# A new order of the opening in a fused linear-attention and feed-forward kernel: two row blocks of w_in ahead of the last pair's loads, and the first q on another queue

## The chip, the cores and the metric

The kernel runs on one NeuronCore of a Trainium2 chip. The metric is the device time of one launch in microseconds (us); lower is better. The kernel before takes 258.86 us, the median of three runs (258.49 to 258.88). Engines are named as the profile names them: PE is TensorE (PEld its weight loads), DVE is VectorE, ACT is ScalarE, POOL is GpSimd, and SP is the engine that does nothing here but issue DMAs.

## The reference, and what is computed

Eight batches of eight heads, 576 rows of 64 elements each, go through a linear attention without softmax; its output is normalised per row and head, and the 4608 rows of 512 go through a two-layer feed-forward net with a gate:

```
kv  = einsum('bhsd,bhse->bhde', k, v)            # 64 x 64 for each head
out = einsum('bhsd,bhde->bhse', q, kv)
x   = out / sqrt(mean(out * out, -1) + 1e-6) * g_norm
h   = x @ w_in                                   # 512 -> 2048
g   = h * sigmoid(1.702 * h)
y   = g @ w_out                                  # 2048 -> 512
```

Inputs and output are f32. The kernel computes in f16 with f32 accumulation in PSUM.

## The kernel before, in words

**Tiles and layers.** The order of all instructions is written out by hand: each engine runs its instructions in program order, and the framework adds the semaphore waits that the data and the buffers need. A batch's 512 features are four *pairs* of heads (128 rows of x each, `NPAIR` = `KO` = 4). The hidden layer of one batch is 16 column blocks of 128 (`FO`), and each is a sum of four matmuls, one for each row block of w_in, that is, one for each pair: `d0.mm(ko, fo)` multiplies row block `ko` of column block `fo` with `x` of pair `ko`, 512 tokens wide (L478). `gate(fo)` then applies the gated activation on ScalarE (L487). The first batch's sixteen columns run in the order `COLS` = 0-3, 8-11, 4, 5, 6, 12, 13, 7, 14, 15. After them `project_all` multiplies with w_out (L822). The later batches (from 46 us on) use a scheme of seven products in place of eight for both layers (L589, L709); the change doesn't touch them.

**The opening.** Batch 0 is not turned by DMA as later ones are, but worked pair by pair. For pair `c`: `q(c)` transposes q on TensorE (twelve small matmuls, L439) and VectorE copies the result out (L445); `kv(c)` forms K transposed times V (twelve matmuls, L261) and VectorE masks it into `kvb` (L429); `out(c)` multiplies both (L307) and ScalarE squares the result (L325, the tile `sq`); `ss(c)` sums the squares over each head with a matmul by ones (L384) and ScalarE takes the reciprocal root (L386, the tile `rs`); `apply(c)` multiplies out, rs and g_norm on VectorE into x (L394). Then the hidden matmuls of row block `c` can run. `busy(n)` issues n matmuls whose result nobody reads (L869). The list of calls from `a0 = First(0)` on (L858 to L923) sets the order on all engines.

**The group.** Hidden matmuls can't be finished before the last pair's x is there. So `GROUP` = 6 columns are begun early, each in a PSUM bank of its own (three of the pool `ps_h`, one of `ps_a`, two of `ps_o`): their row blocks 0 to 2 run while pair 3 is still on its way, then row block 3 and the gate follow for all six. The other ten columns run one after another in banks of `ps_h` (`first_columns`, L804), with other work hung on the positions 6, 7, 8, 12 and 13 of the column order.

**Queues.** Pair 0's k, q and v are loaded as f32 by three DMAs on SP's queue (L161) and cast by DVE, ACT and DVE; the small g_norm comes by ScalarE's queue. All else is loaded by POOL's queue, which casts to f16 on the way: q, k, v of pairs 1, 2, 3 (`early_load`, L91), then w_in in eight DMAs (`load_w_in(f0, f1, k0, k1)`: column blocks f0 to f1 of row blocks k0 to k1, L180), then w_out (L206) and batch 1. The order on this queue is the order of the calls.

Of the kernel before, what the change touches and what calls it, by code (L numbers as in the profile page):

```python
# [7 lines left out]
F16 = mybir.dt.float16  # L8
# [4 lines left out]
P = 128  # L13
# [3 lines left out]
def kernel(  # L17
# [10 lines left out]
    nc = tc.nc  # L28

    B, H, S, D = q.shape  # L30
    DM = H * D
    DFF = moe_w_in.shape[1]
    NPAIR = H // 2
    FO = DFF // P
    KO = DM // P
# [6 lines left out]
    EARLY = 2  # L42
    PE_ = 96
    NJ = S // PE_
    GROUP = 6
    COLS = (0, 1, 2, 3, 8, 9, 10, 11, 4, 5, 6, 12, 13, 7, 14, 15)
    assert PE_ * NJ == S and PE_ % 32 == 0

# [7 lines left out]
    ps_a = ctx.enter_context(tc.tile_pool(name="ps_a", bufs=3, space=bass.MemoryType.PSUM))  # L56
    ps_h = ctx.enter_context(tc.tile_pool(name="ps_h", bufs=3, space=bass.MemoryType.PSUM))
    ps_o = ctx.enter_context(tc.tile_pool(name="ps_o", bufs=2, space=bass.MemoryType.PSUM))
# [28 lines left out]
    def early_src(n, b, c0, c1):  # L87
        return srcs[n][b, 2 * c0 : 2 * c1].rearrange("h (p j) d -> p h (j d)", j=NJ)

    def early_load(n, b, c0, c1):  # L90
        nc.gpsimd.dma_start(  # L91
            out=raw[n][0:PE_, c0:c1, :].rearrange("p c (l x) -> p (c l) x", l=2),
            in_=early_src(n, b, c0, c1),
        )
# [60 lines left out]
    for n in "kqv":  # L155
        if n != "q":
            rows = stage.tile([P, 6, 2 * P], F32, name="qf", tag="qf", bufs=2)
            rows = rows.rearrange("p h x -> p (h x)")[0:PE_]
        first[n] = rows[:, (n == "q") * 2 * NJ * D :][:, 0 : 2 * NJ * D]
        dst, src = first[n].rearrange("p (h x) -> p h x", h=2), early_src(n, 0, 0, 1)  # L160
        nc.sync.dma_start(out=dst, in_=src)  # L161
    g_row = const.tile([1, D], F32)
    nc.scalar.dma_start(out=g_row, in_=g_norm.unsqueeze(0))
    nc.vector.memset(ident, 0.0)
# [2 lines left out]
        out=ident,  # L167
        in_=ident,
# [10 lines left out]
    def load_w_in(f0, f1, k0=0, k1=KO):  # L179
        nc.gpsimd.dma_start(  # L180
            out=w_in_sb[:, k0:k1, f0 * P : f1 * P],
            in_=moe_w_in[k0 * P : k1 * P, f0 * P : f1 * P].rearrange(
                "(ko ki) f -> ki ko f", ki=P
            ),
        )

    for c in range(1, NPAIR):
        for n in "qkv":
            early_load(n, 0, c, c + 1)
    load_w_in(0, 4, 0, 1)  # L190
    load_w_in(0, 4, 1, 2)
    load_w_in(0, 4, 2, 3)
    load_w_in(8, 10)
    load_w_in(0, 4, 3, KO)
    load_w_in(10, 12)
    load_w_in(4, 8)
    load_w_in(12, FO)

    nc.scalar.preload_act_table_set("abs_reciprocal_sqrt_and_small")
    nc.vector.memset(eps_t, EPS)  # L200
# [220 lines left out]
    class First(Early):  # L421
# [10 lines left out]
                ones2.rearrange("p (l d) -> p l d", l=2),  # L432
            )

        def q(self, c):
            t = ps_h.tile([P, S], F16, name="q0", tag="hT")
            for j in range(NJ):
                for hl in range(2):
                    nc.tensor.transpose(  # L439
                        t[hl * D : (hl + 1) * D, j * PE_ : (j + 1) * PE_],  # L440
                        qraw[0:PE_, c, (hl * NJ + j) * D : (hl * NJ + j + 1) * D],
                        ident[0:PE_, 0:PE_],
                    )
            s = attn.tile([P, S], F16, name="qT", tag="qT", bufs=4)
            nc.vector.tensor_copy(s, t)  # L445
            self.qT[c] = s
# [340 lines left out]
    def layers(t, units1, units2):  # L787
        hid = d0 if t == 0 else Hidden(t)
        seven = Seven(t, hid.gT) if t else None
        left = hid_seven(t, hid, seven, units1) if t else first_columns(hid, units1)  # L790
        osbs[t] = opool.tile([P, 4, DM], F32, name="osb", tag="osb")
        if t:
            todo = {n: [lambda x=x: seven.sums(*x) for x in xs] for n, xs in plan(t).later.items()}
            for n, us in units2.items():
                todo.setdefault(n, []).extend(us)
            for n, us in left.items():
                todo[n] = us + todo.get(n, [])
            seven.run(todo)
        else:
            project_all(hid.gT, units2)  # L800
        if EARLY <= t < B and t not in HALVED:
            store(t, 0, J)

    def first_columns(hid, units):  # L804

        for i, fo in enumerate(COLS):
            if i >= GROUP:
                for ko in range(KO):
                    hid.mm(ko, fo)
                hid.gate(fo)  # L810
            for u in units.get(i, ()):
                u()
# [45 lines left out]
    a0 = First(0)  # L858
# [8 lines left out]
    def busy(n):  # L867
        for _ in range(n):
            nc.tensor.matmul(  # L869
                idle_ps,  # L870
                kvb[1][:, 0, :],
                kvb[1].rearrange("p c r -> p (c r)"),
                start=True,
                stop=True,
            )
# [14 lines left out]
    a0.kv(1)  # L890
    a0.ss(0)
    a0.out(1)
    a0.q(2)
    busy(1)
    a0.kv(2)
    a0.ss(1)
    a0.apply(0)
    a0.out(2)
    a0.q(3)
    a0.apply(1)  # L900
    d0 = Hidden(0)
    busy(3)
    a0.kv(3)
    a0.ss(2)
    a0.apply(2)
    d0.mm(0, 0)
    d0.mm(0, 1)
    a0.out(3)
    d0.mm(0, 2)
    d0.mm(0, 3, ps_a, "att")  # L910
    for fo in range(4):
        d0.mm(1, fo)
        if fo == 1:
            a0.ss(3)
            a0.apply(3)
    for fo in range(4):
        d0.mm(2, fo)
    for fo in COLS[4:GROUP]:
        for ko in range(KO - 1):
            d0.mm(ko, fo, ps_o, "o")  # L920
    for fo in COLS[0:GROUP]:
        d0.mm(KO - 1, fo)
        d0.gate(fo)  # L923
# [197 lines left out]
```

## Time and profile before

| | before |
|---|---|
| median of three runs | 258.86 us (258.49 to 258.88) |
| span of the profiled execution, first to last instruction | 256.5 us |
| own time of the profiled execution | not listed beside the three runs; the median is 2.4 us above its span |
| PE busy | 250.5 us (98%) |
| DVE, ACT, POOL busy | 194.4, 177.0, 57.8 us |
| granted TensorE clock over the span | 1.000 |
| moved by DMA | 35.33 MB, 138 GB/s in the mean |

In the profile a row of the timeline gives start and length in us, the engine, the line, the operation, out<-in, the shape, how many instructions were merged, and in brackets the idle time before it with what ended that. A row of DMA issues gives the size of one and the median time from issue to landing; asked for a stretch that holds a single issue, it is that one's time. The length of a matmul includes its pipeline: one of 512 columns shows as 0.38 while the next can start 0.216 us after it. In the chain of work that ended last each piece is what the end had to wait for, and lines of TensorE there mean that TensorE itself was the bound.

### The profile page before, as it was taken

To read this page: it belongs to the slowest core of one execution; us is meant where nothing else is said; L and a number is where in the kernel's file an instruction comes from. 1 tells how busy PE (TensorE), PEld (TensorE's weight loads), DVE (VectorE), ACT (ScalarE), POOL (GpSimd) and SP (SyncE) were. 2 spreads that over 40 slices of the span, in tenths; PEclk is the share of its full clock that TensorE was granted. 3 is DMA by queue.
4 is the path that set the end of the run, shared out by engine and by line. 5 is a ranking of instruction groups with operands and counts; after the bars stand their busy time and mean duration, and the time that the engine had idled before them with its cause. 6 is when DMAs were issued, how large, how long until landed. Compare 5 with 4: busy or idle time off the path is not lost.

```text
span 256.5 us, 6359 instructions
## 1 busy us (share of the span) xinstructions
PE 250.5 (98%) x2600; PEld 203.8 (79%) x2600; DVE 194.4 (76%) x341; ACT 177.0 (69%) x322; POOL 57.8 (23%) x94
## 2 busy tenths in 40 slices
PE   7899999999999999999999999999999999999994
PEld 2444544788888888888888888888888889888883
DVE  1557585999958895989588867986899687857872
ACT  3469725978759885989598958995798569537800
POOL 8882155404080104301340143000000000000013
PEclk9999999999999999999999999999999999999999
DMA  7999999998999989998999699909500730012005
GB/s 180 189 201 205 205 204 196 191 178 128 165 183 214 118 115 172 216 273 109 211 170 137 87 228 128 177 4 156 184 4 0 93 155 3 0 75 91 3 19 146
DMA packets 68703, 35.33 MB, mean 138 GB/s; under 512 B 37986, under 2 KB 66274, under 8 KB 68418
## 3 DMA queue, kind: packets, MB, share of 16 engines
q0 software_dynamic: 37648, 18.31, 55.4%
q1 hardware_dynamic: 30624, 16.29, 28.7%
q8 instruction: 20, 0.33, 0.6%
q10 hardware_dynamic: 402, 0.33, 0.4%
q14 instruction: 9, 0.07, 0.1%
HBM read 36.70 MB, written 9.44 MB: 180 GB/s over the span
## 4 chain that ended last, share of the span: by engine, by line
PE 94%; DMA 2%; POOL 2%; DVE 0%; issue 0%
PE o L709 38%; PE h L589 38%; PE o L822 5%; PE hT L478 5%; DMA vbuf<-in_v_dram 2%; PE kvp L248 2%; PE outR L337 1%; PE ss L384 1%; POOL qraw L91 1%; PE outT L307 1%; POOL kraw L91 0%; PE q L459 0%; PE kvp L261 0%; PE idle L869 0%; PE kv L261 0%; PE outT L311 0%
## 5 line engine op out<-in xcount | busy, mean ns | idle before, releaser
L566 ACT ACTIVATE gT<-h 128x512 f16<-128x512 f32 x96 | 52.4, 602 | 5.7 <-PE h L589 5.7
L589 PEld LDWEIGHTS <-ws 128*128 128x128 f16 x512 | 50.0, 98 | 6.0
L709 PEld LDWEIGHTS <-gS 128*128 128x128 f16 x512 | 49.0, 98 | 6.2 <-DVE gS L641 0.3
L589 PE MATMUL h<-xS,ws 128*128 128x256 f16 x384 | 52.2, 273 | 0.0
L709 PE MATMUL o<-tw,gS 128*128 128x256 f16 x384 | 45.6, 273 | 0.0
L589 PEld LDWEIGHTS <-w_in_sb 128*128 128x128 f16 x384 | 37.5, 98 | 4.7
L709 PEld LDWEIGHTS <-gT 128*128 128x128 f16 x384 | 37.6, 98 | 4.3
L709 PE MATMUL o<-w_out_sb,gT 128*128 128x256 f16 x256 | 31.4, 273 | 0.0
L589 PE MATMUL h<-xT,w_in_sb 128*128 128x256 f16 x224 | 31.1, 272 | 0.0
L603 DVE TENSOR_TENSOR h<-h,s 128x512 f32<-128x512 f32 x32 | 22.3, 698 | 4.4 <-PE h L589 2.8
L605 DVE TENSOR_TENSOR s<-h,s 128x512 f32<-128x512 f32 x32 | 22.1, 691 | 4.3 <-PE h L589 3.5
L686 DVE TENSOR_TENSOR osb<-o,qf 128x512 f32<-128x512 f32 (+1 forms) x25 | 16.7, 668 | 11.2 <-PE o L709 11.1
L743 POOL DMA_DIRECT2D out_dram<-osb x6 | 3.2, 538 | 93.2 <-DVE osb L686 93.2
L641 DVE TENSOR_TENSOR gS<-gT 128x512 f16<-128x512 f16 (+2 forms) x32 | 21.3, 684 | 0.6 <-ACT gT L566 0.6
L566 ACT ACTIVATE gT<-s 128x512 f16<-128x512 f32 x32 | 19.8, 628 | 2.8 <-DVE s L605 2.8
L589 PE MATMUL h<-xS,w_in_sb 128*128 128x256 f16 x128 | 18.9, 273 | 0.0
L353 DVE TENSOR_REDUCE sum<-sq 128x8 f32<-128x512 f16 x24 | 14.9, 679 | 4.7 <-ACT sq L347 4.7
L995 ACT ACT_TABLE_LOAD x14 | 18.0, 1283 | 0.3
L535 DVE COPY s<-h 128x512 f32<-128x512 f32 x19 | 13.0, 685 | 6.5 <-PE h L589 6.4
L325 ACT ACTIVATE sq<-outT 128x512 f16<-128x512 f32 (+1 forms) x16 | 7.8, 493 | 14.3 <-PE outT L307 8.7
L115 POOL DMA_DIRECT2D kraw<-in_k_dram x7 | 6.0, 855 | 49.1 <-PE kvp L248 32.5
L386 ACT ACTIVATE rs<-ss,eps_t 128x512 f32<-128x512 f32 (+1 forms) x16 | 9.2, 581 | 11.2 <-PE ss L384 11.2
(105 smaller groups left out, 372.2 us busy)
## 6 DMA issues: line engine op xcount, KB each, us to landing
out_dram<-osb SPq DMA_DIRECT2D x8, 512.0 KB, 5.4
kraw<-in_k_dram POOLq DMA_DIRECT2D x5, 512.0 KB, 6.0
vbuf<-in_v_dram POOLq DMA_DIRECT2D x5, 512.0 KB, 10.0
out_dram<-osb SPq DMA_DIRECT2D x2, 1024.0 KB, 4.1
qraw<-in_q_dram POOLq DMA_DIRECT2D x3, 512.0 KB, 11.0
qbuf<-in_q_dram POOLq DMA_DIRECT2D x3, 512.0 KB, 12.8
out_dram<-osb SPq DMA_DIRECT2D x6, 192.0 KB, 6.7
w_in_sb<-in_moe_w_in_dram POOLq DMA_DIRECT2D x2, 512.0 KB, 9.6
```

The lines of the kernel that those rows point to most:

```text
L353: nc.vector.tensor_reduce(out=self.sum4[:, j, :], in_=self.o[j][1].rearrange("p (x d) -> p x d", d=D), op=ALU.add, axis=mybir.AxisListType.X,)
L478: nc.tensor.matmul(self.h[fo], w_in_sb[:, ko, fo * P : (fo + 1) * P], self.x[:, ko], start=(ko == 0), stop=(ko == KO - 1),)
L535: (nc.vector.tensor_copy if engine == "D" else nc.scalar.copy)(to, src)
L566: nc.scalar.activation(self.gT[:, to, n * TH : (n + 1) * TH], src, AFT.Gelu_apprx_sigmoid)
L589: nc.tensor.matmul(bank[name][:, a], w, x, start=(p in (1, 5) and a == 0 and k == 0), stop=(k == KH - 1), skip_group_check=True,)
L603: nc.vector.tensor_add(bank["z"], bank["x"], self.s5)
L605: nc.vector.tensor_add(self.s5, bank["x"], self.s5)
L641: op(s[:, n, lo], a, b)
L686: nc.vector.tensor_add(o, ps, self.kept[with_][:, m])
L709: nc.tensor.matmul(o, a, w, start=(p in (1, 2, 5) and i == 0 and (mo == 0 or split)), stop=(i == HF - 1), skip_group_check=True,)
L822: nc.tensor.matmul(os[mo], gT[:, fo, mo * P : (mo + 1) * P], w_out_sb[:, fo, :], start=(fo == 0), stop=(fo == FO - 1),)
L995: u2.setdefault(i, []).append(lambda: f(*args))
```

## The change

Six things change, all in the first batch:

- q of pair 0 is asked for on ScalarE's queue instead of SP's, so that k and v alone are on SP's.
- On POOL's queue, row blocks 0 and 1 of w_in's first four columns go ahead of q, k, v of pair 3 instead of behind them.
- The rest of w_in is cut otherwise: columns 8 to 11 come in four DMAs of one row block (before, two DMAs of all four row blocks for two columns each), with row block 3 of the first four columns between the third and fourth; columns 4 to 7 and 12 to 15 come in two DMAs of two row blocks each (before, one each). w_in takes twelve DMAs instead of eight.
- The calls of the opening stand in another order: `apply(0)` and `apply(1)` one step earlier, `kv(3)` and `out(3)` behind hidden matmuls of row blocks 0, 1 and in part 2, and the four fillers `busy(1)` and `busy(3)` are gone; `q(3)` uses a bank of `ps_o`.
- `GROUP` is 7: seven columns have their row blocks 0 to 2 done before row block 3 of any. The banks are three of `ps_h`, two of `ps_a`, two of `ps_o`.
- Positions 9 and 10 of the column order (`MORE`) use banks of `ps_o`.

What is computed stays the same.

```diff
-    GROUP = 6
+    GROUP, MORE = 7, (9, 10)
...
-        nc.sync.dma_start(out=dst, in_=src)
+        (nc.scalar if n == "q" else nc.sync).dma_start(out=dst, in_=src)
...
     for c in range(1, NPAIR):
+        if c == NPAIR - 1:
+            load_w_in(0, 4, 0, 1)
+            load_w_in(0, 4, 1, 2)
         for n in "qkv":
             early_load(n, 0, c, c + 1)
-    load_w_in(0, 4, 0, 1)
-    load_w_in(0, 4, 1, 2)
     load_w_in(0, 4, 2, 3)
-    load_w_in(8, 10)
+    for k0 in range(KO - 1):
+        load_w_in(8, 12, k0, k0 + 1)
     load_w_in(0, 4, 3, KO)
-    load_w_in(10, 12)
-    load_w_in(4, 8)
-    load_w_in(12, FO)
+    load_w_in(8, 12, 3, KO)
+    for f0 in (4, 12):
+        load_w_in(f0, f0 + 4, 0, 2)
+        load_w_in(f0, f0 + 4, 2, KO)
...
-        def q(self, c):
-            t = ps_h.tile([P, S], F16, name="q0", tag="hT")
+        def q(self, c, pool=ps_h, tag="hT"):
+            t = pool.tile([P, S], F16, name="q0", tag=tag)
...
             if i >= GROUP:
+                pool = (ps_o, "o") if i in MORE else (ps_h, "hT")
                 for ko in range(KO):
-                    hid.mm(ko, fo)
+                    hid.mm(ko, fo, *pool)
                 hid.gate(fo)
...
     a0.out(1)
+    a0.apply(0)
     a0.q(2)
-    busy(1)
+    a0.ss(1)
     a0.kv(2)
-    a0.ss(1)
-    a0.apply(0)
-    a0.out(2)
-    a0.q(3)
-    a0.apply(1)
     d0 = Hidden(0)
-    busy(3)
-    a0.kv(3)
-    a0.ss(2)
-    a0.apply(2)
     d0.mm(0, 0)
     d0.mm(0, 1)
-    a0.out(3)
+    a0.out(2)
+    a0.apply(1)
     d0.mm(0, 2)
     d0.mm(0, 3, ps_a, "att")
-    for fo in range(4):
+    d0.mm(1, 0)
+    a0.ss(2)
+    a0.q(3, ps_o, "o")
+    for fo in range(1, 4):
         d0.mm(1, fo)
-        if fo == 1:
-            a0.ss(3)
-            a0.apply(3)
+    a0.apply(2)
+    a0.kv(3)
     for fo in range(4):
         d0.mm(2, fo)
-    for fo in COLS[4:GROUP]:
-        for ko in range(KO - 1):
-            d0.mm(ko, fo, ps_o, "o")
+        if fo == 1:
+            a0.out(3)
+    d0.mm(0, COLS[4], ps_o, "o")
+    d0.mm(0, COLS[5], ps_a, "att")
+    a0.ss(3)
+    a0.apply(3)
+    for ko in range(1, KO - 1):
+        for fo in COLS[4:6]:
+            d0.mm(ko, fo)
+    for ko in range(KO - 1):
+        d0.mm(ko, COLS[6], ps_o, "o")
     for fo in COLS[0:GROUP]:
         d0.mm(KO - 1, fo)
         d0.gate(fo)
```

## The prediction, made before the changed kernel was run

> **What bounds the kernel now.** I read the page first, then busy time by stretch, then the chain of work that ended last, then the timeline of each engine over the first 30 us. The page and the stretches:
>
> ```profile
> span 256.5 us, 6359 instructions
> PE 250.5 (98%) x2600; PEld 203.8 (79%) x2600; DVE 194.4 (76%) x341; ACT 177.0 (69%) x322; POOL 57.8 (23%) x94
> PEclk9999999999999999999999999999999999999999
> ...
> 9.40:13.80 4.40, 3.87 (x56) 1.88 (x56) 2.68 (x6) 2.35 (x4) 3.80 (x6) 1.00 1.28 199
> 13.80:28.20 14.40, 14.40 (x71) 6.51 (x71) 9.37 (x17) 11.53 (x20) 6.65 (x10) 1.00 1.30 203
> 28.20:46.20 18.00, 18.00 (x146) 8.90 (x145) 11.87 (x27) 10.03 (x16) 8.16 (x12) 1.00 1.34 201
> ```
>
> (In a row by stretch: from:to, its length, then PE, PEld, DVE, ACT, POOL busy us, the granted clock, the DMA share, GB/s.) TensorE is full from 13.8 us on. So the change can only win what the time before 13.8 wastes, and can lose if it opens a hole after it. The chain at the joint:
>
> ```profile
> 5.28 5.54 DMA vbuf<-in_v_dram
> ...
> 15.71 5.62 PE hT L478 x26
> ...
> 21.45 6.95 PE hT L478 x32
> 28.40 1.08 PE o L822 x5
> ```
>
> V of pair 2 lands at 5.28 + 5.54 = 10.82 and starts the full stretch; a hidden-layer matmul costs 5.62 / 26 = 0.216 us. TensorE's timeline:
>
> ```profile
> 9.45 0.39 PE L307 MATMUL outT<-qT,kvb 128*128 128x512 f16 x1
> ...
> 10.15 0.39 PE L869 MATMUL idle<-kvb 128*128 128x512 f16 x1
> 10.95 0.38 PE L261 MATMUL kv<-vbuf,kraw 96*64 96x64 f16 x12 [0.42 <-DMA vbuf<-in_v_dram]
> ...
> 12.41 0.82 PE L869 MATMUL idle<-kvb 128*128 128x512 f16 x3
> ...
> 13.81 0.61 PE L478 MATMUL hT<-xT,w_in_sb 128*128 128x512 f16 x2
> ...
> 15.54 5.79 PE L478 MATMUL hT<-xT,w_in_sb 128*128 128x512 f16 x26
> ```
>
> The first hidden matmul starts at 13.81. Two, then four, then a run of 26 from 15.54: the 22nd is the 16th of that run, at 15.54 + 15 x 0.217 = 18.79. After it 42 more follow without a hole. This 22nd is my yardstick: in the changed order it is the first that needs the last pair's x (21 products of three row blocks with seven column blocks come before it), and 43 remain from it in either kernel.
>
> **The change part by part.** *The DMA order.* Landings, from issue plus time to landing, one answer for each issue:
>
> ```profile
> 7.14 0.64 POOL L91 DMA_DIRECT2D vbuf<-in_v_dram  x1
> 7.76 1.13 POOL L180 DMA_DIRECT2D w_in_sb<-in_moe_w_in_dram  x2
> 9.53 0.53 POOL L180 DMA_DIRECT2D w_in_sb<-in_moe_w_in_dram  x1 [0.64 <-DMA qraw<-in_q_dram]
> ...
> vbuf<-in_v_dram POOLq DMA_DIRECT2D x1, 144.0 KB, 5.9
> ...
> w_in_sb<-in_moe_w_in_dram POOLq DMA_DIRECT2D x1, 128.0 KB, 6.0
> ...
> w_in_sb<-in_moe_w_in_dram POOLq DMA_DIRECT2D x1, 128.0 KB, 5.4
> ```
>
> Pair 3's V lands at 7.14 + 5.9 = 13.04, so its three loads took (13.04 - 10.82) / 3 = 0.74 each. The first w_in block lands at 13.76 (0.72 behind), the third at 14.93, so 0.59 for each of the next two. With two blocks ahead: first block 11.55, second 12.13, pair 3's V 12.13 + 2.22 = 14.35, third block 14.95, and the blocks behind it 0.64 each (128 KB at 203 GB/s). All of w_in is 16 such blocks, and with pair 3 it is in at 10.82 + 2.2 + 16 x 0.64 = 23.3, against 23.8 before (the last one is issued at 13.29):
>
> ```profile
> w_in_sb<-in_moe_w_in_dram POOLq DMA_DIRECT2D x1, 512.0 KB, 10.5
> ```
>
> The four extra issues on POOL cost 0.53 each, but POOL has room: the third block's issue at 9.53 waited 0.64 for the landing of a load eight places before it, and that place falls on the same load after the change. What stands behind on this queue (w_out, batch 1) follows the bytes, so it lands 0.4 to 0.5 earlier; where TensorE gains less, none of it is late.
>
> *The opening's new order*, walked with durations of before. ScalarE's and VectorE's rows:
>
> ```profile
> 9.41 0.69 ACT L386 ACTIVATE rs<-ss,eps_t 128x512 f32<-128x512 f32 x1 [0.46 <-PE ss L384]
> 10.00 0.59 ACT L325 ACTIVATE sq<-outT 128x512 f16<-128x512 f32 x1
> ...
> 16.45 1.28 ACT L487 ACT_TABLE_LOAD   x1
> 18.56 4.03 ACT L487 ACTIVATE gT<-hT 128x512 f16<-128x512 f32 x8 [0.83 <-PE hT L478]
> ...
> 12.53 0.46 DVE L445 COPY qT<-q 128x576 f16<-128x576 f16 x1 [0.21 <-PE q L439]
> ...
> 13.59 0.29 DVE L429 TENSOR_TENSOR kvb<-kv,ones 128x128 f16<-128x128 f32 x1
> 14.63 0.75 DVE L394 SCALAR_TENSOR_TENSOR xT<-outT,g_col,rs 128x512 f16<-128x512 f32 x1 [0.75 <-ACT rs L386]
> ```
>
> Until 9.45 nothing differs. apply(0) runs at 10.14 to 10.88, when rs(0) ends (9.41 + 0.69); q(2)'s copy and the kv(2) product behind it on VectorE still end by 11.66. ss(1) goes when its square ends, 10.64, rs(1) 11.06 to 11.75, apply(1) 11.79 to 12.53. Hidden matmuls (0,0) and (0,1), by row block and column, wait for the first block: 11.6. out(2) follows at 12.05, its square ends 13.06, ss(2) 13.11, rs(2) 13.52 to 14.21; meanwhile three more hidden matmuls, and a hole of 0.2. q(3) at 13.33, its copy (0.46) to 14.28, apply(2) 14.29 to 15.04, kv(3)'s product behind it on VectorE to 15.34. Then (2,0) at 15.09, which stands ahead of out(3) on TensorE: out(3) 15.53, its square to 16.55, ss(3) 16.61, rs(3) 17.02 to 17.71, apply(3) to 18.49. What waits remain are filled with products of the fifth to seventh columns; the yardstick goes at 18.54. Gain: 18.79 - 18.54 = 0.25 us.
>
> The four fillers that go (4 x 0.216 = 0.86) are no gain by themselves: they stood in waits, and in this walk waits of some 1.7 us remain between 9.45 and 18.54. With no wait in their place they would give the whole 0.86; that is the far end, and nothing the near one.
>
> *Seven columns in the group, banks in ps_o for two later ones.* The table load follows rs(3) at 17.73 and ends at 19.01 (1.28). Gates then go every 0.49 (8 in 4.03, the last one's own 0.6 included), so the seventh ends at 22.6. Columns 7 and 8 need banks of gates 0 and 1; position 9 needs the fifth gate's bank (21.6, TensorE there at 21.9), position 10 the seventh's (22.6, there at 22.76). Cost zero, covered by 0.15 to 0.3 us; without cover the hole is what it is late by. q(3) in ps_o takes a bank whose kv(2) is long read.
>
> *q on ScalarE's queue.* V's issue on SP moves up one place; g_norm's load and the table load move one behind q's issue on ScalarE, which is idle until q's cast. Does the data come earlier? The casts, the shares by stretch, and the queues from 4.60 to 5.40:
>
> ```profile
> 3.98 0.56 DVE L861 CAST kraw<-qf 96x768 f16<-96x768 f32 x1 [2.75 <-DMA qf<-in_k_dram]
> 5.07 0.83 ACT L860 CAST qraw<-qf 96x768 f16<-96x768 f32 x1 [2.50 <-DMA qf<-in_q_dram]
> 6.16 0.76 DVE L862 CAST vbuf<-qf 96x768 f16<-96x768 f32 x1 [1.63 <-DMA qf<-in_v_dram]
> ...
> 1.80:4.60 2.80, 2.80 (x8) 0.94 (x7) 0.56 (x1) 0.77 (x1) 2.80 (x5) 1.00 0.94 277
> ...
> 6.00:13.00 7.00, 6.29 (x101) 3.28 (x101) 4.01 (x11) 2.95 (x5) 5.89 (x10) 1.00 1.27 189
> ...
> q0 software_dynamic: 110, 0.08, 73.6%
> q1 hardware_dynamic: 82, 0.10, 48.0%
> ```
>
> With one hardware queue the engines ran at 0.94, later at 1.27. If two queues reach that, the 48% of 0.8 us that SP's loads still took beside POOL's would be done before: 0.38 / 1.25 = 0.3 us for every later landing. If not, nothing. The packets are the same, so the only loss I see is K's: sharing with q it lands about when q does, 5.05, which is 1.1 later and still 1.1 ahead of V, behind which its cast was done anyway. Between 0 and 0.3 no row is nearer: I take 0.15.
>
> The Trainium skill, "DMA: Bandwidth & Descriptors", section "Issuing engines are not separate DMA queues", says that such DMAs share the 16 engines and that a second issuing engine saves only the issue time. By it the 0.15 is 0 and the sum 258.6; the low share of 0.94 leaves it open here.
>
> Sum: 0.25 + 0.15 = 0.4 us. The span would go from 256.5 to 256.1. The profiled execution's own time is not given beside the three runs; their median is 2.4 above its span, and I keep that: 258.86 - 0.4 = 258.5.
>
> **The rivals.** *Earlier than that.* q's queue gives its full 0.3, and the first block follows V after 0.59, as its neighbours do, not 0.72: then 0.25 + 0.3 + 0.13 = 0.7, so 258.2. For it: the share of 0.94. Its limit is w_in itself: all landed at 23.3, 18 matmuls (3.9 us) still behind the last pieces, so the stage can't end before 27.3 where it now ends at 28.23, 0.9 earlier: 257.9.
>
> *Slower: pair 3 comes late.* It now stands behind two w_in blocks, and (2,0), which needs the third block, stands ahead of out(3). If these six loads run at the slow pace from 7.2 to 7.7 us and not at that from 13.35 to 13.9,
>
> ```profile
> DMA packets 113, 0.08 MB, mean 158 GB/s; under 512 B 10, under 2 KB 113, under 8 KB 113
> ...
> DMA packets 121, 0.11 MB, mean 195 GB/s; under 512 B 12, under 2 KB 121, under 8 KB 121
> ```
>
> their 4.2 us become 5.2 and the last x comes 1.0 later: 259.5. It decides from a yardstick at 18.8 (even), and is slower by 0.2% from 19.3. Against it: these loads ran at the quick pace before.
>
> *Slower: the clock falls.* The change takes four fillers away, and TensorE does know a slower speed, at its start:
>
> ```profile
> 1.28 4.38 PE L869 MATMUL idle<-kvb 128*128 128x512 f16 x12 [1.28 <-DVE one_t L202]
> ```
>
> Twelve took 4.38 us where 12 x 0.216 is 2.6. If it fell back to that once, 1.8 us are lost: 258.5 + 1.8 = 260.3. It decides at the length of a hole that no row here shows. Against it: 1.00 in every later stretch, over a wait of 0.42 and more; I count 1.0 us of waits from 9.4 to 12.8 where before had 0.9.
>
> The Trainium skill, "TensorE: Matmul & The Clock Gate", "Part 1", has the gate go back to half rate after an idle window of about 3.4 us; the longest hole of my walk is 0.5, so by that rule too it stays open, and the granted 1.00 agrees.
>
> *The change does nothing:* the last x comes at the old time, because each early product is paid for by a later pair; 258.9.
>
> **How the numbers follow.** 0.2% (0.5 us) is about what a measurement of this kernel can tell from no change. My forecast, with the case that nothing moves, lies inside it: 0.45, its own range 258.3 to 259.0. Earlier: 0.35. Pair 3 late: 0.14. Clock: 0.06. So faster 0.35, same 0.45, slower 0.20. The range goes from the w_in limit, with 0.1 for the runs' spread (257.8), to 259.4, just under the late pair's price; outside are the clock, half of the late pair, and a little below: under 2 in 10.
>
> **What the profile after would show.** The first hidden matmul at 11.4 to 11.6, waiting for w_in; the yardstick at 18.4; the first output product (L822 now) at 27.8; TensorE without a hole from 18.4 on; granted clock 1.00; V of pair 0 cast at 5.9 to 6.15 instead of 6.16. I am wrong if the stretch up to the yardstick has other waits than those for the first block, the squares of pairs 2 and 3 and apply(2), or if TensorE waits after it, at positions 9 and 10 first.

## The result, and the profile after

The changed kernel takes **259.52 us** in the median (258.98 to 259.62, six runs) where the kernel before, in the same series, takes 258.56 (258.49 to 258.88, six runs): a ratio of 1.0032 with a 95% interval of 1.0019 to 1.0045. The forecast was 258.5, within 257.8 to 259.4. The change is a little slower instead of a little faster.

The page of the changed kernel: span, busy time of the engines, then shares of the chain that ended last.

```profile
span 257.2 us, 6356 instructions
PE 250.3 (97%) x2596; PEld 203.1 (79%) x2596; DVE 193.8 (75%) x341; ACT 176.9 (69%) x322; POOL 60.1 (23%) x98
...
PE 84%; DMA 11%; POOL 3%; issue 1%; DVE 0%
```

TensorE lost four instructions and 0.2 us of busy time, and yet the span is 0.7 longer: the time went into waits. The chain of the changed kernel, whose columns are start, length and what was waited for, names them:

```profile
5.70 5.98 DMA w_in_sb<-in_moe_w_in_dram
...
14.95 6.96 DMA w_in_sb<-in_moe_w_in_dram
...
22.20 15.24 DMA w_out_sb<-in_moe_w_out_dram
37.48 1.67 PE o L826 x7
```

Before, V of pair 2 opened the full stretch and TensorE was the bound from there. Now three loads are in the chain: w_in's first block (landed 11.68), a later piece of w_in (21.91), and a piece of w_out (37.44), which TensorE needs at 37.48. The same in the timeline of TensorE and, below it, busy time by stretch (from:to, length, then PE, PEld, DVE, ACT, POOL, clock, DMA share, GB/s), after:

```profile
11.72 0.61 PE L481 MATMUL hT<-xT,w_in_sb 128*128 128x512 f16 x2 [0.24 <-DMA w_in_sb<-in_moe_w_in_dram]
...
15.41 0.60 PE L481 MATMUL hT<-xT,w_in_sb 128*128 128x512 f16 x2 [0.23 <-DMA w_in_sb<-in_moe_w_in_dram]
15.85 0.38 PE L310 MATMUL outT<-qT,kvb 128*128 128x512 f16 x1
...
16.93 0.38 PE L387 MATMUL ss<-sq,ones 128*128 128x512 f16 x1
17.25 4.15 PE L481 MATMUL hT<-xT,w_in_sb 128*128 128x512 f16 x18
...
21.36 7.54 PE L481 MATMUL hT<-xT,w_in_sb 128*128 128x512 f16 x32
28.73 1.24 PE L826 MATMUL o<-w_out_sb,gT 128*128 128x512 f16 x5
```

```profile
13.80:24.00 10.20, 9.90 (x67) 4.14 (x62) 6.37 (x11) 7.75 (x15) 7.84 (x11) 1.00 1.21 193
28.73:47.00 18.27, 18.17 (x146) 8.93 (x145) 11.82 (x27) 10.07 (x16) 7.64 (x11) 1.00 1.34 201
```

Before, the row of that run of 32 hidden matmuls was:

```profile
21.32 7.08 PE L478 MATMUL hT<-xT,w_in_sb 128*128 128x512 f16 x32
```

It took 7.08 us before and takes 7.54 now, and the 146 matmuls from the first output product to batch 1's hidden layer took 18.01 before and 18.27 now. Before, TensorE was busy for the whole of 13.8 to 24.0; now 0.30 us are missing.

Four marks are enough for comparing all runs, so the comparisons below use them: the first hidden matmul; Y, the prediction's yardstick (the 22nd hidden matmul); P, the first output product; and H, batch 1's first hidden product. What stands behind H takes about the same time in all of them (256.5 - 46.24 = 210.3 before, 257.2 - 47.00 = 210.2 after; 210.2 to 210.5 in the others but best). Each row is one profiled execution.

| us | first hidden | Y | P | H | w_in all in |
|---|---|---|---|---|---|
| before | 13.81 | 18.80 | 28.23 | 46.24 | 23.81 |
| after | 11.72 | 18.87 | 28.73 | 47.00 | 24.79 |

In this pair of profiles the opening neither won nor lost (Y + 0.07), and 0.7 us went between Y and H, where the prediction saw nothing.

### The profile page after: what moved, and what is told of

Read it like the earlier page. It is cut to its first block, busy times and chain, and to the rows that moved or that the text cites. A ratio compares the mean times of both kernels' runs of the same rounds, so it can differ in the third digit from the quotient of the medians.

```text
span 257.2 us, 6356 instructions
## 1 busy us (share of the span) xinstructions
PE 250.3 (97%) x2596; PEld 203.1 (79%) x2596; DVE 193.8 (75%) x341; ACT 176.9 (69%) x322; POOL 60.1 (23%) x98
## 4 chain that ended last, share of the span: by engine, by line
PE 84%; DMA 11%; POOL 3%; issue 1%; DVE 0%
PE o L712 38%; PE h L592 38%; DMA w_out_sb<-in_moe_w_out_dram 6%; DMA w_in_sb<-in_moe_w_in_dram 5%; PE o L826 3%; PE kvp L251 2%; PE outR L340 1%; POOL w_in_sb L180 1%; PE ss L387 1%; POOL qraw L91 1%; POOL kraw L91 0%; POOL vbuf L91 0%; PE kvp L264 0%; PE outT L310 0%; PE outT L314 0%
## 5 line engine op out<-in xcount | busy, mean ns | idle before, releaser
L538 ACT COPY h<-h 128x512 f32<-128x512 f32 x27 | 15.4, 577 | 2.1 <-PE h L592 1.8
```

The source lines that it names most:

```text
L538: (nc.vector.tensor_copy if engine == "D" else nc.scalar.copy)(to, src)
```

## The experiments

**One execution is not enough.** The marks move between executions of one kernel, so both kernels were run again, unchanged.

> The kernel before once more, for the spread of one execution. Theory D (the loads' landings vary by some tenths of a us from one execution to the next, and the profile of before was a quick one): span 256.6 to 257.2, the 22nd hidden matmul 0.1 to 0.4 us later than the 18.80 of the first profile, and no wait of TensorE between it and 46 us. If landings don't vary, span 256.5 and 18.8 again.

The kernel before again: 258.59 us (10 runs) beside 258.69 (27 runs), ratio 0.9998 [0.9986, 1.0009]. Its second profile has Y at 19.01, P at 28.47, H at 46.48, each some 0.2 later than in the first. It got there by another way: its first hidden matmul started at 13.31, half a us earlier than in the first profile, but then TensorE waited for the load of columns 8 and 9, which landed at 17.01:

```profile
15.04 1.46 PE L478 MATMUL hT<-xT,w_in_sb 128*128 128x512 f16 x6
17.05 4.49 PE L478 MATMUL hT<-xT,w_in_sb 128*128 128x512 f16 x20 [0.55 <-DMA w_in_sb<-in_moe_w_in_dram]
```

In the first profile that load landed at 16.80 and was used at 16.84. So the kernel before, too, has one early load of w_in that is used as it lands.

> The changed kernel once more. Theory A (the cut: twelve smaller DMAs for w_in are delivered more slowly) and theory B (the order and the second hardware queue make all loads late from the start) both expect the landings of the first profile within 0.2 us (last of w_in at 24.8, w_out of blocks 10 and 11 at 37.4), three waits of TensorE for DMA of 0.16, 0.28 and 0.26 us behind 21 us, and a span near 257.2. Theory C (the slow stretch near 21 us was an accident of that execution) expects one or more of the three waits to be gone and the span 0.2 to 0.5 us shorter.

The changed kernel again: 259.07 (12 runs) beside 258.76, ratio 1.0015 [0.9998, 1.0031], so in this series the loss is smaller and not clear of nothing. Its profile shows the same kinds of wait, larger. TensorE, then the same two stretches:

```profile
1.28 5.30 PE L873 MATMUL idle<-kvb 128*128 128x512 f16 x12 [1.28 <-DVE one_t L205]
6.51 0.69 PE L442 MATMUL q<-ident,qraw 96*64 96x96 f16 x12
...
15.66 0.61 PE L481 MATMUL hT<-xT,w_in_sb 128*128 128x512 f16 x2 [0.22 <-DMA w_in_sb<-in_moe_w_in_dram]
...
25.11 0.61 PE L481 MATMUL hT<-xT,w_in_sb 128*128 128x512 f16 x2 [0.32 <-DMA w_in_sb<-in_moe_w_in_dram]
...
37.96 1.67 PE L826 MATMUL o<-w_out_sb,gT 128*128 128x512 f16 x7 [0.30 <-DMA w_out_sb<-in_moe_w_out_dram]
```

```profile
13.80:24.00 10.20, 9.98 (x70) 4.56 (x70) 6.15 (x11) 7.65 (x14) 7.66 (x11) 1.00 1.21 189
29.01:47.48 18.47, 18.17 (x146) 8.89 (x145) 11.82 (x27) 10.07 (x16) 7.66 (x11) 1.00 1.34 201
```

The first two rows show something else that differs between executions: the twelve fillers took 4.38 before and 5.30 here, and q's twelve transposes 0.69 where pair 2's take 0.45. TensorE ran at half speed to about 7.3 us here, and to 4.6 in the first profile of before. The waits for w_in at 15.66 and 25.11 and for w_out at 37.96 are there a second time, then, with other sizes. A third profile

> The changed kernel, a third profile. Theory Q: slow stretches at 10 to 11.5 and 20.5 to 22 us for the third time, w_in's end at 24.8 or later, w_out of blocks 10 and 11 at 37.4 or later. Theory D: one or both may be missing, with w_in's end from 23.9.

gave 258.65 us in its one run, Y 18.91, P 28.30, H 46.68: there is no wait for w_in's last pieces in it (all in at 23.96), and still one for w_out (H - P 18.38).

**Is it how w_in is cut?** Theory A: twelve DMAs deliver more slowly than eight. Two runs undo it from either side. The kernel before with the change's cut, and the changed kernel with two of the cuts taken back:

```diff
 # before_cut: the kernel before
-    load_w_in(8, 10)
+    for k0 in range(KO - 1):
+        load_w_in(8, 12, k0, k0 + 1)
     load_w_in(0, 4, 3, KO)
-    load_w_in(10, 12)
-    load_w_in(4, 8)
-    load_w_in(12, FO)
+    load_w_in(8, 12, 3, KO)
+    for f0 in (4, 12):
+        load_w_in(f0, f0 + 4, 0, 2)
+        load_w_in(f0, f0 + 4, 2, KO)
 # coarse: the changed kernel
-    for f0 in (4, 12):
-        load_w_in(f0, f0 + 4, 0, 2)
-        load_w_in(f0, f0 + 4, 2, KO)
+    load_w_in(4, 8)
+    load_w_in(12, FO)
```

> The kernel before with w_in cut into the twelve DMAs of the change, and nothing else (pair 3 first, q on SP's queue, the old opening). Theory A: w_in ends at 24.6 or later instead of 23.8, TensorE waits 0.5 to 0.9 us for DMA behind 17 us, and the time rises by 0.5 to 0.8 us. Theory B: w_in ends at 23.8 or earlier, the time is within 0.2 us of before.

> The changed kernel with the last two column groups of w_in in one DMA each, as before (ten DMAs for w_in instead of twelve). Theory A: w_in ends at 24.1 to 24.4 instead of 24.8, the waits behind 21 us shrink from 0.69 to 0.4 us or less, and the time falls by 0.3 us or more. Theory B: w_in ends at 24.8, no change in time beyond 0.2 us.

The kernel before with the fine cut: 258.58 (12 runs), ratio 1.0001 [0.9991, 1.0012]; w_in all in at 23.80. The changed kernel with the coarse tail: 259.42 (12 runs), 1.0034 [1.0006, 1.0061]; Y 19.40, P 28.86, H 46.87, all in at 24.43. Three of these twelve executions, at 261.4 to 261.7 us, have a mean granted clock of 0.993; the other nine have a median of 258.89. The cut costs nothing in the kernel before, and taking part of it back in the changed kernel gives no gain that stands clear of the spread: theory A is out.

**Is it q on ScalarE's queue?** Theory Q: it slows what comes behind. Again from both sides.

```diff
 # q_on_sp, q_on_sp2: the changed kernel
-        (nc.scalar if n == "q" else nc.sync).dma_start(out=dst, in_=src)
+        nc.sync.dma_start(out=dst, in_=src)
 # before_q_act: the kernel before
-        nc.sync.dma_start(out=dst, in_=src)
+        (nc.scalar if n == "q" else nc.sync).dma_start(out=dst, in_=src)
```

> The changed kernel with q of pair 0 back on SP's queue. Theory A: q and V of pair 0 land 0.1 to 0.3 us earlier, w_in still ends at 24.6 to 24.9 and the time is within 0.2 us of the changed kernel's. Theory B: w_in ends at 24.3 or earlier and the time is 0.4 us or more lower.

> The kernel before with q of pair 0 on ScalarE's queue, and nothing else. Theory Q (the second hardware queue is what makes the DMA engines slow from 10 to 11.5 us, as in all three profiles that had it and not in the two that had not): GB/s below 170 in some half us between 10 and 12 us, w_in's end 0.5 us or more later than 23.8, time up by 0.3 to 0.6 us. Theory D: no such stretch more than in the kernel before, time within 0.2 us of before; K of pair 0 lands near 5.0 in either.

> The changed kernel with q on SP's queue, a second profile. Theory Q: again no slow stretch from 10 to 11.5 and from 20.5 to 22 us, w_in's end at 23.9 to 24.2. Theory D: slow stretches come at either place from execution to execution; w_in's end anywhere from 23.9 to 25.

With q back on SP the changed kernel takes 259.04 (12 runs), ratio 1.0017 [1.0006, 1.0028], beside 259.07 with q on ScalarE in the same series. The kernel before with q on ScalarE takes 258.78 (10 runs), 0.9998 [0.9988, 1.0008]. Theory Q is out; q's queue is worth nothing either way. The casts after, which the prediction wanted earlier:

```profile
5.01 0.56 DVE L865 CAST kraw<-qf 96x768 f16<-96x768 f32 x1 [3.78 <-DMA qf<-in_k_dram]
5.34 0.83 ACT L864 CAST qraw<-qf 96x768 f16<-96x768 f32 x1 [2.23 <-DMA qf<-in_q_dram]
6.25 0.56 DVE L866 CAST vbuf<-qf 96x768 f16<-96x768 f32 x1 [0.67 <-DMA qf<-in_v_dram]
```

```profile
1.80:4.60 2.80, 2.80 (x8) 0.94 (x7) 0.00 (x0) 1.28 (x1) 2.80 (x6) 1.00 0.93 263
```

K is 1.03 later than in the first profile of before (5.01 for 3.98), q 0.27 and V 0.09 later (1.47, 0.84 and 0.64 later than in the second), and the share of the DMA engines in 1.8 to 4.6 is 0.93 where it was 0.94. A second queue brought no bandwidth. The rule weighed in the prediction (the Trainium skill, "DMA: Bandwidth & Descriptors", "Issuing engines are not separate DMA queues") is what the trace shows here. The three profiles without the slow tail, again2 and the two with q on SP (the second, a single run, took 258.66), have P at 28.27 to 28.42, as before has.

**The DMA order alone, with the old calls.** The kernel before, with the two blocks ahead of pair 3:

```diff
     for c in range(1, NPAIR):
+        if c == NPAIR - 1:
+            load_w_in(0, 4, 0, 1)
+            load_w_in(0, 4, 1, 2)
         for n in "qkv":
             early_load(n, 0, c, c + 1)
-    load_w_in(0, 4, 0, 1)
-    load_w_in(0, 4, 1, 2)
```

> The kernel before with row blocks 0 and 1 of w_in's first columns loaded ahead of pair 3, and nothing else: the old order of calls, in which kv(3) stands ahead of all hidden matmuls. By the walk (all theories): kv(3) waits for V of pair 3, 14.4 instead of 13.2, with TensorE idle, the 22nd hidden matmul comes 1.0 to 1.4 us later than before, and so does the end. If pair 3's place in the queue didn't matter, no change.

259.83 us (6 runs), ratio 1.0052 [1.0026, 1.0077]. Both halves of the change belong together: the old calls ask for pair 3's q before any hidden matmul. TensorE, and two stretches, in an execution of 261.42 us (four of the six kept their clock, and took 259.39 to 259.88):

```profile
13.76 0.45 PE L440 MATMUL q<-ident,qraw 96*64 96x96 f16 x12 [1.36 <-DMA qraw<-in_q_dram]
14.14 1.46 PE L870 MATMUL idle<-kvb 128*128 128x512 f16 x3
```

```profile
9.40:14.15 4.75, 3.13 (x58) 1.52 (x53) 2.06 (x5) 2.67 (x5) 3.15 (x6) 1.00 1.18 171
14.15:17.57 3.42, 3.42 (x23) 1.24 (x20) 1.62 (x4) 0.69 (x1) 2.82 (x4) 0.50 1.39 197
```

Here the prediction's clock rival is seen. After a stretch in which TensorE was busy for 3.13 of 4.75 us, its longest wait 1.36, the granted clock fell to 0.50 for 3.42 us; that is half of 3.42, 1.7 us, of TensorE's work.

**Is it the supply of w_in?** The theory left: the changed order uses blocks 0 and 2 as they land, so their lateness is paid. The test takes bytes away: blocks 0 to 2 of the first four columns are loaded for two of the four columns, and the others are zero.

```diff
-            load_w_in(0, 4, 0, 1)      # and (0, 4, 1, 2), (0, 4, 2, 3) likewise
+            load_w_in(0, 2, 0, 1)
...
     nc.vector.memset(eps_t, EPS)
+    nc.vector.memset(w_in_sb[:, 0:3, 2 * P : 4 * P], 0.0)
```

> The changed kernel, but row blocks 0 to 2 of w_in's columns 2 and 3 are not loaded; they are set to zero in SBUF (so these two hidden columns lack three quarters of their sum). The three early w_in loads are half as long, 0.3 us each. Theory D (the chain of the walk is right and the late landing of w_in's row blocks 0 and 2 held it up): matmul (2,0) starts at 14.8 to 15.1, set by apply(2), the 22nd hidden matmul at 18.2 to 18.5, and the time is 0.4 to 0.9 us below the changed kernel's. Theory W (the walk is too short, the landings don't matter): the 22nd stays at 18.8 or later, and the time within 0.2 us of the changed kernel's.

258.18 us (10 runs), ratio 0.9982 [0.9972, 0.9992]: 0.9 below the changed kernel's 259.07, and the only variant of it below the kernel before. The blocks land at 10.85, 11.14 and 13.69, and the waits for w_in are gone:

```profile
11.37 0.38 PE L388 MATMUL ss<-sq,ones 128*128 128x512 f16 x1 [0.43 <-ACT sq L329]
11.68 0.38 PE L265 MATMUL kv<-vbuf,kraw 96*64 96x64 f16 x12
11.99 0.61 PE L482 MATMUL hT<-xT,w_in_sb 128*128 128x512 f16 x2
...
15.49 0.59 PE L482 MATMUL hT<-xT,w_in_sb 128*128 128x512 f16 x2
```

Of what was expected, the time came and the marks did not: (2,0) is at 15.49 and Y at 18.94, no earlier than after's. Full speed came only at 7.25 in this execution, and the opening is 0.3 late without a wait for w_in. Y - first hidden is 6.95 (the prediction's walk: 18.54 - 11.6 = 6.94), but again2, with all its bytes, has 6.97, so this profile doesn't show a gain at Y. Behind Y there is no wait: P 28.34, H 46.35. With 192 KB less to load (half of three loads of 128 KB) the time falls, so the supply of loads is what holds the changed kernel back; all later loads come earlier too, and which of them matters this run doesn't tell.

**Does the load of w_out matter?** Batch 1's first K load moved behind the late w_out load, alone and with q on SP:

```diff
-    early_load("k", 1, 0, 2)
...
     load_w_out(10, 12)
+    early_load("k", 1, 0, 2)
```

> The changed kernel with one load moved on POOL's queue: K of batch 1's first two pairs behind w_out's blocks 10 and 11 instead of ahead of w_out's blocks 8 and 9. Theory E (behind the 22nd hidden matmul the loss is w_out's blocks 10 and 11 landing at 37.1 to 37.9, later than the output products want them): they land at 35.6 to 36.6, the wait of 0.26 to 0.46 us near 37 us is gone, the stage from the first output product to the first product of batch 1's hidden layer is 18.0 us again, and the time falls by 0.2 to 0.4 us. Rival: V and K of batch 1, still behind, become what is waited for at 38 to 40 us, and the time stays within 0.1 us.

> The same with q of pair 0 on SP's queue. Theory E: first output product at 28.2 to 28.4, first product of batch 1's hidden layer at 46.2 to 46.5 as in the kernel before, time within 0.2 us of before. Rival: 46.6 or later, time 0.2 us or more above before.

The load lands at 34.89 instead of 37.44 and the wait is gone:

```profile
28.99:47.00 18.01, 18.01 (x146) 8.90 (x145) 11.83 (x27) 10.07 (x16) 8.35 (x13) 1.00 1.34 201
```

But the time is 259.5 (12 runs), 1.0043 [1.0021, 1.0066]; with q on SP 258.97 (12 runs), 1.0005 [0.9989, 1.0021]. In the profile of k_late P is already at 28.99, since block 2 landed at 15.93 and Y came at 19.60. With q on SP it was worse, Y 20.05:

```profile
16.59 0.61 PE L481 MATMUL hT<-xT,w_in_sb 128*128 128x512 f16 x2 [1.15 <-DMA w_in_sb<-in_moe_w_in_dram]
17.03 0.38 PE L310 MATMUL outT<-qT,kvb 128*128 128x512 f16 x1
```

So the w_out wait is real in the trace and its removal is not confirmed in the time.

**Does out(3) have to stand behind (2,0)?** Theory F: with out(3) right behind kv(3), pair 3 no longer depends on block 2. Alone, and with both edits above:

```diff
     a0.kv(3)
+    a0.out(3)
     for fo in range(4):
         d0.mm(2, fo)
-        if fo == 1:
-            a0.out(3)
```

> The changed kernel with out(3) two matmuls earlier, ahead of (2,0), so that pair 3 no longer stands behind the landing of w_in's row block 2. Theory F (in all profiles so far the 22nd hidden matmul came 3.45 to 3.8 us behind (2,0), whose start is the landing of that block: 15.3 to 16.5 instead of the predicted 14.95): out(3) at 15.4 to 15.7 whatever the block does, the 22nd at 18.4 to 18.8, time 0.1 to 0.5 us below the changed kernel's. Rival: TensorE, held at (2,0) anyway, comes to the 22nd no earlier (18.9 or later) and the time stays.

> The same with q of pair 0 on SP's queue and K of batch 1's first pairs behind w_out's blocks 10 and 11. Theory F: 22nd at 18.4 to 18.8, first output product at 27.9 to 28.3, no wait near 37 us, time at or up to 0.4 us below the kernel before. Rival: the 22nd at 18.9 or later, time at or above before.

259.51 (12 runs), 1.0035 [1.0013, 1.0057], and 259.5 (12 runs), 1.0023 [1.0007, 1.0039]. The profile of the first, where block 2 landed at 15.56:

```profile
15.72 0.39 PE L310 MATMUL outT<-qT,kvb 128*128 128x512 f16 x1 [0.38 <-DVE kvb L432]
15.94 1.46 PE L481 MATMUL hT<-xT,w_in_sb 128*128 128x512 f16 x6
17.24 0.38 PE L387 MATMUL ss<-sq,ones 128*128 128x512 f16 x1
```

out(3) goes ahead of (2,0), but it waits for kv(3)'s product on VectorE until 15.72, only 0.13 earlier than after (15.85) and later than block 2's landing. Then ss(3) stands behind six hidden matmuls and comes at 17.24 (after: 16.93), Y at 19.18. In the second profile four of these six wait for block 2, which landed at 16.81, and Y is at 20.10. Theory F in this form fails; moving ss(3) too was not tried.

**Earlier loads for pair 1.** Two attempts at a version that beats both: pair 1's loads asked for before POOL builds its constants, in the kernel before; and all together in the changed kernel.

```diff
 # pool_first; best is the changed kernel with this, q on SP and the coarse tail
+    for n in "qkv":
+        early_load(n, 0, 1, 2)
     nc.gpsimd.affine_select(...)
...
-    for c in range(1, NPAIR):
+    for c in range(2, NPAIR):
```

> The kernel before, with the three loads of pair 1 issued on POOL ahead of the setting up of ident and ones2 (they start 0.8 us earlier), and nothing else. Theory D (the landings of w_in set when the first batch ends, in the old opening too): w_in ends 0.2 to 0.4 us earlier, the first output product comes at 28.0 or earlier, and the time falls by 0.1 to 0.4 us. If the loads are bound by the pace of the 16 engines from 2 us on whatever is issued first, nothing changes beyond 0.1 us.

> The changed opening with q on SP's queue, the last two column groups of w_in in one DMA each, and pair 1's loads issued on POOL ahead of ident and ones2. Theory D: first w_in block at 11.3 to 11.6, the 22nd hidden matmul at 18.5 to 18.8, at most 0.2 us of waits behind it, time 0.1 to 0.4 us below the kernel before. If the slow stretches of w_in's loads come in this order too: the 22nd at 19.0 or later, time 0.2 us or more above before.

260.42 (12 runs), 1.0076 [1.0047, 1.0105], and 261.14 (8 runs), 1.0097 [1.0062, 1.0131]. POOL's first load goes out at 1.35 instead of 1.79, 0.44 earlier and not 0.8. In the profiled execution of pool_first (262.50 us) V of pair 0, on which everything waits, is cast at 8.79 instead of 6.16, and V of pair 1 itself lands at 9.70 instead of 8.05:

```profile
9.40 0.38 PE L263 MATMUL kv<-vbuf,kraw 96*64 96x64 f16 x12 [2.68 <-DVE vbuf L864]
```

```profile
4.75:11.57 6.82, 4.02 (x63) 2.07 (x61) 1.69 (x6) 1.43 (x2) 5.06 (x10) 1.00 1.20 195
11.57:18.40 6.83, 6.83 (x59) 2.84 (x59) 3.06 (x8) 2.60 (x5) 6.01 (x9) 0.50 1.23 167
```

The clock fell again, now for 6.83 us; six of the twelve executions have a mean granted clock of 0.993 or less. Why V is late is not shown. The profile of best is of an execution with a span of 522.7 us, twice that of the others, so no cause is read from it. No variant that does the whole work beat the kernel before.

## Why the prediction was wrong

Each row is one profiled execution; blocks 0 and 2 are the first and third load of w_in, and (2,0) is the hidden matmul of row block 2 and column 0. "Six loads" is the time from the landing of pair 2's V to that of block 2: in either order these six are pair 3's q, k and v and w_in's blocks 0 to 2.

| us | block 0 in | block 2 in | six loads | (2,0) | Y | w_in all in | P - Y | H - P |
|---|---|---|---|---|---|---|---|---|
| predicted | 11.55 | 14.95 | 4.13 | 15.09 | 18.54 | 23.3 | 9.4 | as before |
| before | 13.76 | 14.95 | 4.13 | 15.97 | 18.80 | 23.81 | 9.43 | 18.01 |
| base_again | 13.26 | 14.56 | 4.21 | 15.48 | 19.01 | 24.03 | 9.46 | 18.01 |
| after | 11.68 | 15.36 | 4.51 | 15.41 | 18.87 | 24.79 | 9.86 | 18.27 |
| again | 12.05 | 15.62 | 5.25 | 15.66 | 19.12 | 25.07 | 9.89 | 18.47 |
| again2 | 11.90 | 15.40 | 5.04 | 15.44 | 18.91 | 23.96 | 9.39 | 18.38 |
| coarse | 11.96 | 15.54 | 5.05 | 15.58 | 19.40 | 24.43 | 9.46 | 18.01 |
| k_late | 11.98 | 15.93 | 5.44 | 15.97 | 19.60 | 24.39 | 9.39 | 18.01 |
| q_on_sp | 11.60 | 15.52 | 4.59 | 15.57 | 19.03 | 23.93 | 9.39 | 18.17 |
| sp_k_late | 12.05 | 16.54 | 5.86 | 16.59 | 20.05 | 25.05 | 9.40 | 18.01 |

**What held.** The walk from (2,0) on: Y - (2,0) was 3.45 in the prediction (18.54 - 15.09), and is 3.45 to 3.47 in five of the seven rows of the changed order; in coarse (3.82) and k_late (3.63) TensorE waits once more, for the load behind block 2, in at 16.97 and 17.17. (0,0) waits for w_in in after, as said. Nothing waits at positions 9 and 10 for a bank, so the seven columns and `MORE` cost nothing. The table load goes right behind rs(3). In the profiled execution of the changed kernel the granted clock is 1.00 throughout, with the four fillers gone.

**The step that failed: the landings, 0.25 us.** The prediction moved the loads at the steps of before ("first block 11.55, second 12.13 [...] third block 14.95"). In the changed order the same six loads took 4.5 to 5.9 us instead of 4.1: block 0 came at 11.60 to 12.05 and block 2 at 15.36 to 16.54. In after, (2,0) is 15.41 - 15.09 = 0.32 late, and the yardstick 18.87 - 18.54 = 0.33. Of the 0.32, 0.10 is that apply(2) ended at 15.14 instead of 15.04, behind a first hidden matmul at 11.72 instead of 11.6, and 0.22 is the wait for block 2, behind which out(3) stands too. In again and again2 apply(2) itself ended at 15.52 and 15.36, and block 2 adds 0.1 or less; there the first hidden matmul came at 12.10 and 11.94, in again2 behind a wait for block 0, in again with no wait of TensorE's, whose full speed came late, at 7.3. The mean Y of the three profiles of the changed kernel is 18.97, and of before (18.80, 19.01) 18.91: the 0.25 is gone.

The prediction's rival "pair 3 comes late" had this mechanism: "their 4.2 us become 5.2", and the six loads took 4.51, 5.25 and 5.04 in the three profiles of the changed kernel. Its 259.5 is the measured median by luck: it put 1.0 us on the last x, where 0.33 came in after and was about as much as the gain, and the rest of the loss lies behind the yardstick; and a second series of the same kernel gave 259.07. One sign of being wrong that the prediction named is in the profile after, the wait of (2,0) for w_in, and so is the other, waits behind the yardstick, though not at positions 9 and 10.

**The second failure: "none of it is late", behind the yardstick.** w_in was to be in at 23.3; it was in at 23.9 to 25.1, and before at 23.8 and 24.0. Two waits follow. For w_in's last pieces: P - Y 9.86 and 9.89 against 9.43 before, in two of the three profiles, 0.45 us. For the w_out load of columns 10 and 11: H - P 18.27, 18.47, 18.38 against 18.01, 0.26 to 0.46 us. Together they are 0.3 to 0.9; H is 47.00, 47.48 and 46.68 against 46.24 and 46.48, and the times (259.52 and 259.07 against some 258.6) differ by as much. Part of H's delay in `again` is the late full speed of that execution. In the variants of the changed order P - Y is 9.39 to 9.46, so the wait for w_in's last pieces is not in every execution.

**Why loads of the same bytes come later** is only in part settled. That the order brings it is shown: in the five profiles with pair 3 ahead of w_in the six loads take 4.13 to 4.21 us, in the eleven with blocks 0 and 1 first and all bytes loaded (best left out) 4.51 to 6.02, and before_order, which changes nothing but this order, has the 6.02. Part of it is that reads are slower near 10 us. The stretch 9.90 to 11.60 (columns as above) after, in before and in before_order:

```profile
9.90:11.60 1.70, 1.16 (x26) 0.67 (x25) 1.19 (x3) 1.24 (x3) 1.29 (x3) 1.00 1.20 173
```

```profile
9.90:11.60 1.70, 1.28 (x26) 0.66 (x24) 0.69 (x3) 0.69 (x2) 1.41 (x3) 1.00 1.31 199
```

```profile
9.90:11.60 1.70, 1.63 (x28) 0.83 (x27) 0.72 (x3) 1.18 (x2) 1.29 (x2) 1.00 0.98 133
```

All five profiles with pair 3 first have 199 or 200 GB/s there; of the twelve with blocks 0 and 1 first, light_w among them, eleven have 133 to 178, and q_on_sp has 196. q's queue is not needed for it, since before_order has q on SP's. Why these reads are slower at this place stays open. A second slow stretch, 20.50 to 22.00, comes in five of the twelve and in none of the five; after, then before:

```profile
20.50:22.00 1.50, 1.50 (x12) 0.56 (x10) 0.74 (x2) 1.50 (x4) 1.12 (x2) 1.00 1.17 170
```

```profile
20.50:22.00 1.50, 1.50 (x12) 0.77 (x11) 0.63 (x1) 1.50 (x5) 0.15 (x1) 1.00 1.24 208
```

170 GB/s for 208 over 1.5 us is 57 KB, or 0.3 us, of w_in.

Beside this, single loads come late in either order, and a packet of instructions that travels among the data is one likely reason. The queues from 14.95 to 15.20 after, and from 14.2 to 14.4 before (packets, MB, and the sum of the packets' times as a share of 16 engines, which passes 100% where packets overlap):

```profile
q0 software_dynamic: 52, 0.05, 115.7%
q8 instruction: 1, 0.02, 24.4%
```

```profile
q0 software_dynamic: 64, 0.03, 124.7%
q8 instruction: 1, 0.02, 29.2%
```

One packet takes 24.4% of 16 engines for 0.25 us, that is 0.98 us of one engine. In sixteen of the eighteen profiles one such packet falls at 14.0 to 15.2, in pool_first and best at 16.2 and 15.5. In thirteen of the sixteen a load near it takes 0.35 to 1.25 us longer than the usual 0.64 for 128 KB, in the other three 0.2 or less. In the kernel before it is the load of columns 8 and 9, in at 16.80 and 17.01; in the changed order it is block 2 or a load behind it. Another packet falls at 33.2 to 36.2. In the five profiles with a wait for w_out it comes while that load is in flight; but in out3_first and light_w it does so too, and there the load takes 1.39 and 1.23 us, near the 1.30 of before. The Trainium skill, "Runtime: NRT & Kernel Launch", "Instruction fetch mechanics", has instructions fetched in blocks of 16 KiB over a DMA queue; the changed kernel's page agrees (20 packets, 0.33 MB, 16.5 KB each):

```profile
q8 instruction: 20, 0.33, 0.6%
```

That the packet is a cause rests on when it comes; no run moved it alone, and it is not the whole cause.

How much a late load costs depends on its reserve, the time from landing to first use. In before, block 2 had 1.0 (in at 14.95, used at 15.54 + 2 x 0.217 = 15.97), and the load of columns 8 and 9 had none. In the changed order block 0 and block 2 are used within 0.05 of their landings wherever TensorE is there in time.

**The 0.15 us for q's queue** was nothing: the low share of 0.94 was not a limit of one queue, and stays 0.93 with two. The prediction had the rule that said so beside it, and 258.6 as its sum.

**The starting point.** "Their median is 2.4 above its span, and I keep that" was off by 0.6: the run whose profile was taken after was 258.98 with a span of 257.2, 1.8 apart, and in the others it was 1.7 to 1.8. So the profile of before was of a run of about 258.3, quicker than the median, and its marks were early ones: with nothing changed, base_again's Y is 0.21 later. That is nearly the whole 0.25 that was to be won.

**The clock rival** (0.06) did not set the profile, but it is not empty: two of the first six timed executions of the changed kernel, none of the next twelve, three of twelve of coarse, two of k_late, four of out3_first and one of out3_sp_k have a mean granted clock of 0.993 or just below, which in before_order is one stretch of 3.42 us at half clock; none of some hundred executions of the kernel before has. In the first series the two took 259.52 and 259.62, and the other four have a median of 259.5, so it isn't the loss; the medians of coarse and out3_first without theirs are 258.9 and 259.2.

**A sum that doesn't come out.** The w_in limit of the range, 23.3 + 3.9, is 27.2 and not 27.3; the range moves by 0.1 at its lower end, and nothing else hangs on it.

## What to carry to other kernels

An order that puts a load's first use right at its landing has no reserve, and pays for every late load; the kernel before had one such load, the changed one two or three. Don't take the time of a load in one order for its time in another: here the same six loads took 4.1 us in one and 4.5 to 6.0 in the other. Count, for each load that a change moves, the time from landing to first use, and set it against the spread of landings in two or three profiles of the same kernel (here, over three executions of the changed kernel, 0.4 us for the first block of w_in and 1.1 us for its last piece) before any gain of 0.3 us is believed. Bytes that are moved ahead push others back, and what stands at the tail of the queue (here w_in's last pieces, and w_out 20 us later) has to be walked as closely as the opening. Where a gain of 0.2% is at stake, measure the kernel before's own spread first.

## What the runs showed of the hardware beside this

- The granted clock falls on waits that are short one by one: after 3.13 busy us in 4.75 with a longest wait of 1.36 (before_order), and after 4.02 busy in 6.82 with one of 2.68 (pool_first); in the last 3.4 us ahead of the fall TensorE was busy for 1.99 and 2.04. The clock stays at 0.50 for 3.42 and 6.83 us, once and twice the same length. The Trainium skill, "TensorE: Matmul & The Clock Gate", "Part 1", asks for an idle window of some 3.4 us; the length agrees, and a stretch that is only partly idle was enough here.
- TensorE reaches full speed at 4.3 to 7.3 us, and this differs between executions of one kernel (4.5, 6.3 and 7.3 for the changed kernel, 4.6 and 5.4 for the one before); the twelve fillers from 1.28 took 4.35 to 5.30 us.
- With POOL's loads of pair 1 issued 0.44 us earlier beside SP's (pool_first, one profile), the product that waits for V of pair 0 went at 9.40 instead of 6.98.
